# A two-layer attention and spectral kernel: who does the work at a layer's end, in which order ScalarE runs the loop, and when weights are split

## The chip, the cores and the metric

The kernel runs on one core of a Trainium2 chip. The metric is the device time of one execution in microseconds (us), as the median of several runs. The engines are PE (TensorE, matmuls), DVE (VectorE), ACT (ScalarE), POOL (GpSimd) and SP (SyncE, which here issues the DMAs).

## What is computed

Two layers, each an attention block and then a spectral block, both with a layer norm ahead and a residual added. The sequence has 2048 rows, the model 1024 columns, 32 heads of 32 columns.

```python
def _A_ref(x, wqkv, wo):                      # attention
    qkv = (x @ wqkv).reshape(B, S, 3, H, Dh) ...
    scores = einsum("bhqd,bhkd->bhqk", q, k) * (Dh ** -0.5)
    p = softmax(scores)
    o = einsum("bhqk,bhkd->bhqd", p, v)
    return o.transpose(...).reshape(B, S, D) @ wo
def _B_ref(x, w_r, w_i):                      # spectral filter
    X = rfft2(x) * (w_r + 1j * w_i)
    return irfft2(X)
x = A_x
for _ in range(2):
    x = x + _A_ref(_layernorm(x), A_wqkv, A_wo)
    x = x + _B_ref(_layernorm(x), B_w_r, B_w_i)
```

## The kernel before, in words

**Precision.** Matmuls of projections and scores take f16 pairs: a value is split into hi (ScalarE, a scaled cast, L166) and lo (VectorE, the rest, L167), and three products hi·hi, hi·lo, lo·hi are summed. `split` (L164) does both.

**The prologue of a layer** normalizes 16 tiles of 128 rows (`ln_tile`), transposes and splits them into `big`, and projects the first V, K and Q groups.

**The loop** (L608 on) runs over 8 groups g of four heads, 4 chunks c of 512 queries, 16 key tiles kt. A step computes the scores of four heads into two PSUM tiles (`S`, L540) and two exponentials of 128x1024 (L544, ScalarE). Every second step multiplies two tiles of exponentials into the output (`PV`, L550). VectorE adds the exponentials up (`add`, L561 and L563), since the sums are the softmax's denominators. After a chunk's last key tile `fin` sums over partitions (L569, PE), transposes, takes reciprocals and scales the output (L570 to L576, VectorE), and at kt = 5 of the next chunk `out` casts it (L582, ScalarE), takes the rest (L583, GpSimd) and stores both halves to `od` in DRAM (SP).

**Beside it** the projections of the next groups fill PE's free time: `filler` (L386) yields in slices, and each sum, of 24 matmuls (`qk_chunk`, L327) or more (`v_tiles`, L371), ends with a split or a copy. A phase's weights are loaded and split by `prep` (L231): slices of 256 KB by DMA into a buffer of three (`wst`), two slices for a Q or K group, four for a pair of V groups. Each is split (L253) and in layer 0 also searched for its largest magnitude (L256, L257, VectorE). `filler` advances `prep` by one slice behind each sum. In the last two groups the filler is the output projection: `load_wo` splits `wo` in 16 slices (into `big`), `wo_parts` computes the first 7 of 8 groups' part of the rows.

**Who sets the order.** PE's order in the loop and at the layer's end is that of the source (`manual_schedule`, L607). The other engines' instructions are put in order by a scheduler at build time, which may move a cast or a weight split ahead of exponentials that stand before it in the source. Engines then run their instructions strictly in that order.

**The layer's end** (L656 on). Rows 0 to 1535 (tiles 0 to 11) have their last eighth added in `wo_rest`, whose statistics are gathered in `mvs`; `fold_rests` normalizes them all. The last chunk's four tiles (`first`, `last`) wait for the loop's last `fin` and `out`: their last eighth is multiplied by `olast`. Each normalized tile is folded: sums and differences of its two halves of rows' columns (`fold`, L141; two operations of 128x8x8x8, GpSimd), ready for the first transposes of the spectral block (`t1`, L742). The inverse root of the variance (`ln_scale`, L116) is one power on GpSimd (L120) and five small operations on VectorE, one of them ahead of the power (L119), four behind (a Newton step, L121 to L124). `norm_folded` then normalizes the folded tile in two halves (L160, L161; VectorE). So for tiles 0 to 11: 24 folds on GpSimd, 24 halves normalized on VectorE.

**The flags.** In layer 1 the kernel reduces its range flags over all partitions (`partition_all_reduce`, L1088, GpSimd), an operation whose code is not resident: GpSimd's order has an exchange of code before and after it. The same holds for the largest norms of each group in the loop (L352).

Of the kernel before, what the change touches and what calls it, by code (L numbers as in the profile page):

```python
# [6 lines left out]
F32 = mybir.dt.float32  # L7
# [4 lines left out]
AF = mybir.ActivationFunctionType  # L12
ALU = mybir.AluOpType
# [99 lines left out]
    return st  # L113


def ln_scale(nc, sm, cst, mv, n=1):  # L116

    v, r, q = (sm.tile([128, n], F32, name=f"{c}{n}") for c in "vrn")
    nc.vector.tensor_scalar(v, mv[:, 1::2], 1e-5, None, op0=ALU.add)  # L119
    nc.gpsimd.tensor_tensor(r, v, cst["mhalf"].broadcast_to([128, n]), op=ALU.pow)  # L120
    nc.vector.tensor_mul(q, r, r)  # L121
    nc.vector.tensor_mul(q, q, v)
    nc.vector.tensor_scalar(q, q, -0.5, 1.5, op0=ALU.mult, op1=ALU.add)
    nc.vector.tensor_mul(r, r, q)  # L124
    return r


def ln_stats(nc, sm, cst, st, mv):

    nc.vector.bn_aggr(mv, st)  # L130
    return ln_scale(nc, sm, cst, mv)


def layernorm(nc, sm, cst, x, out):
# [3 lines left out]
    nc.vector.tensor_scalar(out, x, mv[:, 0:1], r, op0=ALU.subtract, op1=ALU.mult)  # L138


def fold(nc, x, out, a):  # L141

    xv = x.rearrange("p (a u g q) -> p g a u q", a=8, g=2, q=8)[:, :, a]
    ov = out.rearrange("p (u g a q) -> p g a u q", g=2, a=8, q=8)[:, :, a]
    nc.gpsimd.tensor_tensor(ov[:, 0], xv[:, 0], xv[:, 1], op=ALU.add)
    nc.gpsimd.tensor_tensor(ov[:, 1], xv[:, 0], xv[:, 1], op=ALU.subtract)


def fold_norm(nc, sm, cst, st, out):

    mv = sm.tile([128, 2], F32, name="mv")
    r = ln_stats(nc, sm, cst, st, mv)
    b = sm.tile([128, 1], F32, name="b")
    nc.vector.tensor_scalar(b, mv[:, 0:1], 2.0, None, op0=ALU.mult)
    norm_folded(nc, out, out, b, r)


def norm_folded(nc, x, out, b, r):
    xv, ov = (a.rearrange("p (u g q) -> p g u q", g=2, q=64) for a in (x, out))
    nc.vector.tensor_scalar(ov[:, 0], xv[:, 0], b, r, op0=ALU.subtract, op1=ALU.mult)  # L160
    nc.vector.tensor_scalar(ov[:, 1], xv[:, 1], r, None, op0=ALU.mult)  # L161
# [8 lines left out]
def run(g):  # L170
    for _ in g:
        pass
# [89 lines left out]
SPILL = [2, 3, 8, 9]  # L262
# [3 lines left out]
def attention(nc, tc, layer, ap, xin, yd, wts, wo, cst, dram, flags):  # L266
# [5 lines left out]
    pp, qp, sgp, wqp, wvp = ap.pp, ap.qp, ap.sgp, ap.wqp, ap.wvp  # L272
    sq, on, on2, sm = ap.sq, ap.on, ap.on2, ap.sm
# [14 lines left out]
    V, K, Q, bias, nrm, mx = {}, {}, {}, {}, {}, {}  # L288
# [106 lines left out]

# [68 lines left out]
    wo_dst = [ap.x[:, 10 + t if t in SPILL else t] for t in range(8)] + [None] * 2 + [ap.x[:, t] for t in (10, 11)]  # L464
# [12 lines left out]
    mvs = sm.tile([128, 24], F32, name="mvs")  # L477

    def wo_rest(t):
        p = psS.tile([128, 2, 512], F32, name="s")  # L480
        nc.vector.bn_aggr(mvs[:, 2 * t:2 * t + 2], wo_last(t // 4, t % 4, p, wo_dst[t], wo_dst[t], True))
# [12 lines left out]

    vk = [v_tiles(PH0[0], t) for t in range(8)]
    xn = [ln_tile(0), ln_tile(1)]
# [14 lines left out]
    for c in range(NCH):  # L511
        t = 4 * c + 4
# [91 lines left out]
                yield sums - (i + m >= steps)  # L604
            sums -= 1

    with tc.manual_schedule(engines={mybir.EngineType.PE}):  # L607
        for g in range(NG):  # L608
            todo = sum(sums(ph) for ph in beside.get(g, []))
            sl = slots(fill, todo, 22 if g == NG - 2 else 32, 24)  # L610
# [1 line left out]
            for u in range(NCH * NKT):  # L612
# [26 lines left out]
                elif g == NG - 1:  # L639
                    t = rests[0] if rests else 16  # L640
# [15 lines left out]
        run(wof)  # L656
        for t in rests:
            wo_rest(t)
        ps, xs = [], []
# [16 lines left out]
        fold_rests()  # L676
        first(1, range(7))
        last(0)
        first(2, range(7))
        last(1)  # L680
        first(3, range(4))
        last(2)
        first(3, range(4, 7))
        last(3)
# [494 lines left out]
```

## Time and profile before

| what | us |
|---|---|
| median of 3 runs (lowest, highest) | 4022.38 (4021.28, 4024.88) |
| the profiled execution's own time | 4029.87 |
| its span, first to last instruction | 4028.0 |
| layer 0: loop, end | 130 to 1680, 1680 to 1760 |
| layer 1: loop, end | 2130 to 3675, 3675 to 3762 |

The mean granted TensorE clock is 0.982. PE's busy time in stretches is 1502.4 of 1545 us in layer 1's loop, 52.8 of 80 us at layer 0's end and 54.7 of 87 us at layer 1's end. A row of a timeline gives the start, the duration, the engine, the line, the operation, output and inputs, and in brackets the engine's idle time before it and what ended that. A row of a view of waits gives an engine, the tile and line that it was about to work on, the engine, tile and line that it waited for, and total, number and longest of the waits. A row of a view by line gives total and mean (ns) behind the bar, then the idle time before them.

### The profile page before, as it was taken

The numbers are of one execution on the slowest core, as the hardware profiler recorded it, in microseconds if no ns is written. First come the engines' busy times: TensorE is split into PE (matmuls) and PEld (weight loads), VectorE is DVE, ScalarE is ACT, GpSimd is POOL, SyncE is SP. The second block draws the span as 40 slices with busy tenths as digits, with TensorE's granted clock in tenths as the row PEclk, the third lists the DMA queues.
The fourth block names the chain that finished last, engine by engine and source line by source line (L and its number), as shares of the span: only waits on it lengthen the run. The fifth ranks groups of instructions, "written<-read, shape, count | busy, mean of one in ns | idle before, by whom it ended". The sixth has DMA issues, their size and how long they took to land. (4 is left out here: it accounts for less than half of the span.)

```text
span 4028.0 us, 80149 instructions
## 1 busy us (share of the span) xinstructions
PE 3791.8 (94%) x33204; PEld 1680.2 (42%) x33204; DVE 3257.1 (81%) x3897; ACT 2863.0 (71%) x3533; POOL 634.9 (16%) x585
## 2 busy tenths in 40 slices
PE   7999999999999999979989999999999999997898
PEld 5322423342234233368854234233422432332787
DVE  6789888888988977766766898888889889788456
ACT  4677777787778866448746787788878888663485
POOL 1111011101110100314321110111011101003143
PEclk9999999999999999989989999999999999999999
DMA  3000000000000211143120000000000002121333
GB/s 114 19 22 17 7 22 14 14 9 22 17 12 7 87 51 66 53 152 125 57 84 14 27 17 7 22 17 14 7 22 17 12 9 87 53 72 49 141 101 100
DMA packets 97561, 177.32 MB, mean 44 GB/s; under 512 B 7201, under 2 KB 52897, under 8 KB 96161
## 3 DMA queue, kind: packets, MB, share of 16 engines
q1 hardware_dynamic: 97040, 172.03, 12.7%
q8 instruction: 262, 4.29, 0.5%
q14 instruction: 115, 0.93, 0.1%
q10 hardware_dynamic: 144, 0.07, 0.0%
HBM read 123.83 MB, written 48.23 MB: 43 GB/s over the span
## 5 line engine op out<-in xcount | busy, mean ns | idle before, releaser
L544 ACT ACTIVATE p<-s,bias 128x1024 f32<-128x1024 f32 x2048 | 2163.9, 1111 | 534.6 <-PE s L540 527.9
L563 DVE TENSOR_TENSOR R<-R,p 128x1024 f32<-128x1024 f32 x1792 | 2163.1, 1259 | 163.2 <-ACT p L544 160.7
L550 PE MATMUL o<-p,R 128*32 128x512 f32 x8192 | 996.0, 604 | 0.0
L327 PE MATMUL x<-big,wqk 128*128 128x512 f16 x2880 | 678.6, 380 | 18.0 <-DVE R L167 9.3
L540 PEld LDWEIGHTS <-R 32*128 32x128 f16 x12288 | 239.1, 92 | 845.6 <-issue 728.6
L540 PE MATMUL s<-R 32*128 32x512 f16 x6144 | 444.4, 380 | 49.2 <-ACT p L544 44.4
L540 PE MATMUL s<-Q,R 32*128 32x512 f16 x6144 | 442.2, 378 | 27.8 <-ACT p L544 16.7
L327 PEld LDWEIGHTS <-wqk 128*128 128x128 f16 x3072 | 276.8, 98 | 449.1 <-issue 162.8
L550 PEld LDWEIGHTS o<-p,R 128*32 128x32 f32 x8192 | 214.8, 109 | 529.7 <-issue 529.1
L371 PEld LDWEIGHTS <-big 128*128 128x128 f16 x3072 | 291.9, 98 | 102.3 <-issue 56.3
L371 PE MATMUL x<-wv,big 128*128 128x256 f16 x2688 | 321.1, 275 | 5.9 <-DVE big L167 2.9
L561 DVE SCALAR_TENSOR_TENSOR R<-p 128x1024 f32<-128x1024 f32 x128 | 153.9, 1204 | 195.6 <-ACT p L544 195.6
L331 POOL TENSOR_TENSOR sq<-R 128x512 bf16<-128x512 f16 x96 | 149.3, 1555 | 970.8 <-ACT R L166 970.6
L583 POOL TENSOR_TENSOR ohl<-zt,ohl 128x512 f16<-128x512 f32 x62 | 83.2, 1342 | 1178.4 <-ACT ohl L582 1178.4
L429 PE MATMUL x<-big 128*128 128x512 f16 x1008 | 228.0, 380 | 0.0
L429 PEld LDWEIGHTS <-big 128*128 128x128 f16 x1344 | 126.8, 98 | 177.6 <-issue 35.4
L582 ACT CAST ohl<-zt 128x512 f16<-128x512 f32 x64 | 39.6, 618 | 140.0 <-DVE zt L576 98.6
L861 DVE TENSOR_TENSOR H<-G,H 128x512 f16<-128x512 f32 (+1 forms) x68 | 46.7, 687 | 104.1 <-ACT H L860 104.0
L331 POOL TENSOR_TENSOR sq<-Q 128x512 bf16<-128x512 f16 x32 | 48.9, 1529 | 444.6 <-ACT Q L166 444.6
L813 PE MATMUL ps<-cbi,H 128*128 128x256 f16 (+1 forms) x792 | 99.1, 273 | 5.6 <-ACT H L860 3.7
L806 ACT COPY U<-ps 64x256 f32<-64x256 f32 (+1 forms) x272 | 97.0, 357 | 7.8 <-PE ps L813 2.6
L806 ACT COPY B<-ps 64x256 f32<-64x256 f32 (+1 forms) x272 | 97.0, 356 | 6.7 <-PE ps L813 2.4
(417 smaller groups left out, 3256.3 us busy)
## 6 DMA issues: line engine op xcount, KB each, us to landing
wst<-in_wp SPq DMA_DIRECT2D x96, 256.0 KB, 2.8
R<-y SPq DMA_DIRECT2D x32, 512.0 KB, 5.2
w<-in_w SPq DMA_DIRECT2D x60, 256.0 KB, 2.7
od<-ohl SPq DMA_DIRECT2D x56, 256.0 KB, 2.4
big<-od SPq DMA_DIRECT2D x16, 896.0 KB, 6.4
y<-R SPq DMA_DIRECT2D x20, 512.0 KB, 2.6
R<-in_x SPq DMA_DIRECT2D x16, 512.0 KB, 6.8
wst<-in_wo SPq DMA_DIRECT2D x32, 256.0 KB, 3.1
```

Of the source, the lines that this page charges most:

```text
L327: nc.tensor.matmul(ps, a, b, start=d == 0 and i == 0, stop=d == 7 and i == 2)
L331: nc.gpsimd.tensor_tensor(nrm[ph][:, c], t[:, 0], t[:, 0], op=ALU.mult)
L371: nc.tensor.matmul(ps[:, j], l, r, start=d == 0 and i == 0, stop=d == 7 and i == 2)
L429: nc.tensor.matmul(p, a, b, start=start and d == ds[0] and i == 0, stop=stop and d == ds[-1] and i == 2)
L540: nc.tensor.matmul(s[h // 2][:, h % 2], K[g][r, a, kt * 128:kt * 128 + 128], Q[g][r, b, c * 512:c * 512 + 512], start=i == 0, stop=i == 2)
L544: nc.scalar.activation(p, s[hf], AF.Exp, bias=bias[g], scale=SCALE / (SQ * SQ))
L550: nc.tensor.matmul(O[g, c][32 * h:32 * h + 32], V[g][:, kt, 32 * h:32 * h + 32], P[g, c, kt, h // 2][:, h % 2], start=kt == 0, stop=kt == ...
L561: nc.vector.scalar_tensor_tensor(acc[hf], P[g, c, 0, hf], 1e-34, p, op0=ALU.add, op1=ALU.add)
L563: nc.vector.tensor_add(acc[hf], acc[hf], p)
L583: eng.tensor_tensor(t[:, 1], r, t[:, 0], op=ALU.subtract)
L806: nc.scalar.copy(ov[64 * r:64 * r + 64, a0:a0 + m, x], tl[64 * x:64 * x + 64, :m, r])
L813: nc.tensor.matmul(out, l, r, start=k == 0, stop=k == len(mm_) - 1)
```

## The change

Four things change.

1. `ln_scale` takes the engine. At a layer's end all its operations, with two more for the bias (`scale_bias`), run on GpSimd: eight small ones per call.
2. At a layer's end ScalarE normalizes a whole tile (L498, 128x1024) and VectorE folds the result; for the last four tiles VectorE folds first, then ScalarE normalizes one half (L685) and VectorE the other (L686). `fold_rests` is a generator: six tiles come before `first(1)`, four behind `last(0)`, the rest behind `last(1)`, as far as ScalarE's and VectorE's order goes by the source (PE's alone does at the layer's end).
3. In the loop ScalarE, too, runs in the order of the source: `manual_schedule` takes Activation.
4. Behind the second and each later sum of a phase `filler` advances `prep` twice instead of once, so that splits come in pairs, and a phase's last one comes one sum or more sooner.

```diff
-def ln_scale(nc, sm, cst, mv, n=1):
+def ln_scale(nc, sm, cst, mv, eng, n=1):
     v, r, q = (sm.tile([128, n], F32, name=f"{c}{n}") for c in "vrn")
-    nc.vector.tensor_scalar(v, mv[:, 1::2], 1e-5, None, op0=ALU.add)
+    eng.tensor_scalar(v, mv[:, 1::2], 1e-5, None, op0=ALU.add)
     nc.gpsimd.tensor_tensor(r, v, cst["mhalf"].broadcast_to([128, n]), op=ALU.pow)
...
-def fold(nc, x, out, a):
+def fold(nc, x, out, a, eng=None):
...
             for n in range(sums(ph)):
                 yield from (v_tiles if ph[0] == "v" else qk_chunk)(ph, n)
-                next(nxt, None)
+                for _ in range(1 + (n > 0)):
+                    next(nxt, None)
...
+    def scale_bias(mv, n, m):
+        r = ln_scale(nc, sm, cst, mv, nc.gpsimd, n)
+        b = sm.tile([128, n], F32, name=f"b{n}")
+        nc.gpsimd.tensor_tensor(b, mv[:, 0::2], r, op=ALU.mult)
+        nc.gpsimd.tensor_scalar(b, b, -m, None, op0=ALU.mult)
+        return r, b
+
     def fold_rests():
-        r = ln_scale(nc, sm, cst, mvs, 12)
-        b = sm.tile([128, 12], F32, name="b12")
-        nc.vector.tensor_scalar(b, mvs[:, 0::2], 2.0, None, op0=ALU.mult)
+        r, b = scale_bias(mvs, 12, 1.0)
         for t in SPILL + [t for t in range(12) if t not in SPILL]:
-            o = ap.x[:, t]
-            f = o if t in SPILL else pp.tile([128, 1024], F32, name="xn", tag="p")
-            fold(nc, wo_dst[t], f, slice(0, 8))
-            norm_folded(nc, f, o, b[:, t:t + 1], r[:, t:t + 1])
+            f = pp.tile([128, 1024], F32, name="xn", tag="p")
+            nc.scalar.activation(f, wo_dst[t], AF.Identity, bias=b[:, t:t + 1], scale=r[:, t:t + 1])
+            fold(nc, f, ap.x[:, t], slice(0, 8), nc.vector)
+            yield
...
-    with tc.manual_schedule(engines={mybir.EngineType.PE}):
+    with tc.manual_schedule(engines={mybir.EngineType.PE, mybir.EngineType.Activation}):
...
+    with tc.manual_schedule(engines={mybir.EngineType.PE}):
+        ps, xs, folds = [], [], fold_rests()
...
         def last(t):
             o = ap.x[:, 12 + t]
             st = wo_last(3, t, ps[t], xs[t], xs[t], False)
-            fold(nc, xs[t], o, slice(0, 8))
-            fold_norm(nc, sm, cst, st, o)
+            mv = sm.tile([128, 2], F32, name="mv")
+            nc.vector.bn_aggr(mv, st)
+            r, b = scale_bias(mv, 1, 2.0)
+            fold(nc, xs[t], o, slice(0, 8), nc.vector)
+            ov = o.rearrange("p (u g q) -> p g u q", g=2, q=64)
+            nc.scalar.activation(ov[:, 0], ov[:, 0], AF.Identity, bias=b, scale=r)
+            nc.vector.tensor_scalar(ov[:, 1], ov[:, 1], r, None, op0=ALU.mult)
```

Lines behind the first edits have higher numbers in the new kernel (L166 is L167, L544 is L552, L582 is L590, L145 is L146, L570 is L578, L1088 is L1108).

PE's order is the same in both. On ScalarE, in layer 0's loop, where the four splits of the first V weights (`wv`) of the loop stood before (p is a tile of exponentials, x8 means eight in a row, oc and ohl are a chunk's output):

```order
L166 ACTIVATE wqk<-wst 128x512 x2
L544 ACTIVATE p<-s,bias 128x1024 x2
L166 ACTIVATE wv<-wst 128x4x128
L544 ACTIVATE p<-s,bias 128x1024 x2
L166 ACTIVATE wv<-wst 128x4x128
L544 ACTIVATE p<-s,bias 128x1024 x2
L166 ACTIVATE wv<-wst 128x4x128
L544 ACTIVATE p<-s,bias 128x1024 x2
L166 ACTIVATE wv<-wst 128x4x128
L544 ACTIVATE p<-s,bias 128x1024 x4
```

and where they stand now:

```order
L167 ACTIVATE R<-x 128x512
L552 ACTIVATE p<-s,bias 128x1024 x4
L167 ACTIVATE wv<-wst 128x4x128 x2
L552 ACTIVATE p<-s,bias 128x1024 x6
L562 COPY oc<-o 128x512
L552 ACTIVATE p<-s,bias 128x1024 x2
L167 ACTIVATE R<-x 128x512
L552 ACTIVATE p<-s,bias 128x1024 x4
L167 ACTIVATE wv<-wst 128x4x128 x2
L552 ACTIVATE p<-s,bias 128x1024 x4
L590 CAST ohl<-zt 128x512
```

The four splits followed one pair of `wqk` splits within eight exponentials; now they come in two pairs, each four exponentials behind the end of a sum (R<-x), and nearly a group later. Likewise the pair of splits of the first K weights of the loop, which the scheduler had put into the prologue, now stands behind the loop's first four exponentials.

On VectorE at layer 0's end, around the last chunk's `fin` before (xn and R hold tiles, b and r their bias and root):

```order
L160 TENSOR_SCALAR R<-xn,b_18278,r_18270 128x8x64
L161 TENSOR_SCALAR R<-xn,r_18270 128x8x64
L570 STREAM_TRANSPOSE zt<-s 128x512
L160 TENSOR_SCALAR R<-xn,b_18278,r_18270 128x8x64
L572 RECIPROCAL rc<-zt 128x16
L161 TENSOR_SCALAR R<-xn,r_18270 128x8x64
L573 TENSOR_TENSOR fr<-fr,rc 128x16
L575 STREAM_TRANSPOSE zt<-rc 128x512
L160 TENSOR_SCALAR R<-xn,b_18278,r_18270 128x8x64
L576 SCALAR_TENSOR_TENSOR zt<-oc,zt 128x512
```

and now:

```order
L146 TENSOR_TENSOR R<-xn 128x8x8x8
L147 TENSOR_TENSOR R<-xn 128x8x8x8
L578 STREAM_TRANSPOSE zt<-s 128x512
L146 TENSOR_TENSOR R<-xn 128x8x8x8
L580 RECIPROCAL rc<-zt 128x16
L147 TENSOR_TENSOR R<-xn 128x8x8x8
L581 TENSOR_TENSOR fr<-fr,rc 128x16
L583 STREAM_TRANSPOSE zt<-rc 128x512
L146 TENSOR_TENSOR R<-xn 128x8x8x8
L584 SCALAR_TENSOR_TENSOR zt<-oc,zt 128x512
```

The transpose stood behind 16 halves of a norm (eight tiles), the first of which waited for the root; it now stands behind ten folds (five tiles). Twelve VectorE operations, eleven folds and the lo part of the cast, stand between the product with zt and the first of the last four tiles.

On GpSimd at layer 1's end before (ISA without operands is an exchange of code, fa the flags):

```order
L146 TENSOR_TENSOR xn<-R 128x8x8x8
L1088 ISA
L1088 ISA fa<-f_43236 128x6
L145 ISA
L145 TENSOR_TENSOR R<-xres 128x8x8x8
L146 TENSOR_TENSOR R<-xres 128x8x8x8
L120 TENSOR_TENSOR r_39957<-v_39956,mhalf 128x1
```

and now:

```order
L489 TENSOR_TENSOR b_39935<-mv,r_39927 128x1
L490 TENSOR_SCALAR b_39935<-b_39935 128x1
L1108 ISA
L1108 ISA fa<-f_43236 128x6
L119 ISA
L119 TENSOR_SCALAR v_40016<-mv 128x1
L120 TENSOR_TENSOR r_40017<-v_40016,mhalf 128x1
```

The flags' reduction stood behind the folds of tiles 0 to 11 and ahead of the first of the last four tiles; it now stands between the small operations of the first and of the second of these four. SP's order changes in the same stretch: stores of the last tiles stand between other loads of the spectral block's constants than before.

More of the change, by code (lines that the diff above doesn't have):

```diff
@@ L113, in bn_stats @@
     return st
-def ln_scale(nc, sm, cst, mv, n=1):
+def ln_scale(nc, sm, cst, mv, eng, n=1):
     v, r, q = (sm.tile([128, n], F32, name=f"{c}{n}") for c in "vrn")
-    nc.vector.tensor_scalar(v, mv[:, 1::2], 1e-5, None, op0=ALU.add)
+    eng.tensor_scalar(v, mv[:, 1::2], 1e-5, None, op0=ALU.add)
     nc.gpsimd.tensor_tensor(r, v, cst["mhalf"].broadcast_to([128, n]), op=ALU.pow)
[L121 to L124, printed above, removed]
+    eng.tensor_tensor(q, r, r, op=ALU.mult)
+    eng.tensor_tensor(q, q, v, op=ALU.mult)
+    eng.tensor_scalar(q, q, -0.5, 1.5, op0=ALU.mult, op1=ALU.add)
+    eng.tensor_tensor(r, r, q, op=ALU.mult)
     return r
@@ L670, in last, with some @@
             st = wo_last(3, t, ps[t], xs[t], xs[t], False)
-            fold(nc, xs[t], o, slice(0, 8))
-            fold_norm(nc, sm, cst, st, o)
+            mv = sm.tile([128, 2], F32, name="mv")
[5 more added lines that the diff above has]
+            nc.vector.tensor_scalar(ov[:, 1], ov[:, 1], r, None, op0=ALU.mult)
+        def some(n):
+            for _ in range(n):
+                next(folds, None)
         first(0, range(7))
@@ L675, in attention @@
         out(NG - 1, NCH - 1, nc.vector)
-        fold_rests()
+        some(6)
         first(1, range(7))
         last(0)
+        some(4)
         first(2, range(7))
         last(1)
+        run(folds)
         first(3, range(4))
```

8 lines of the change are left out of this document (4 added, 4 removed).

## The prediction

> **What bounds the kernel now.** I read the page first, then the waits of PE and ACT over each attention loop, then timelines at the places these named. The page's first lines:
>
> ```profile
> span 4028.0 us, 80149 instructions
> PE 3791.8 (94%) x33204; PEld 1680.2 (42%) x33204; DVE 3257.1 (81%) x3897; ACT 2863.0 (71%) x3533; POOL 634.9 (16%) x585
> ```
>
> PE is the bound. Its 54144-instruction order is the same in both kernels, so only PE's idle time, 4028.0 − 3791.8 = 236 us, is to be had. The waits of PE over layer 0's loop (130 to 1680 us; columns: engine, what it was about to do, whom it waited for, total, times, longest):
>
> ```profile
> PE s L540 <- ACT p L544: 31.0, 29, 4.7
> PE s L540 <- DVE mqk L346: 11.3, 7, 3.5
> ```
>
> and over layer 1's loop (2130 to 3675 us):
>
> ```profile
> PE s L540 <- ACT p L544: 29.1, 28, 3.5
> PE s L540 <- DVE mqk L346: 2.8, 4, 0.8
> ```
>
> So 60.1 us go while a score matmul waits for an exponential. What held ScalarE is in its own waits over layer 0's loop:
>
> ```profile
> ACT wv L166 <- DMA wst<-in_wp: 29.8, 12, 5.3
> ACT ohl L582 <- DVE zt L576: 11.8, 8, 3.8
> ```
>
> ScalarE stands in front of a V-weight split whose slice has not landed, and the exponentials queue behind it.
>
> **Part A, the V-weight splits.** One such place, in the timeline at 200 us (start, duration, engine, line, in brackets the idle time and its releaser):
>
> ```profile
> 199.72 0.63 ACT L166 ACTIVATE wv<-wst 128x512 f16<-128x512 f32 x1 [3.75 <-DMA wst<-in_wp]
> 201.40 1.86 PE L540 MATMUL s<-R 32*128 32x512 f16 x12 [3.15 <-ACT p L544]
> ```
>
> ScalarE waits 3.75 us, PE loses 3.15. Six such bursts occur, three in each layer; PE's waits in 25 us around each (195, 575, 960, 2215, 2587 and 2960 us):
>
> ```profile
> PE s L540 <- ACT p L544: 6.4, 3, 3.1
> PE s L540 <- ACT p L544: 5.0, 2, 3.3
> PE s L540 <- ACT p L544: 6.6, 3, 4.7
> PE s L540 <- ACT p L544: 4.8, 3, 3.2
> PE s L540 <- ACT p L544: 5.2, 3, 3.5
> PE s L540 <- ACT p L544: 6.4, 4, 3.5
> ```
>
> Together 34.4 us. In the new order each V split stands where a sum ends, and by the two orders at least 28 exponentials separate the freeing of a staging buffer from the use of what is loaded into it: 29 us by the four in 4.12 us quoted in part C, where the longest wait for a slice was 5.3. I take the whole −34.4. The DMA's own queue is SP, where the load stands behind an `od` store that waits for the cast six exponentials later than before; 28 exponentials cover that, too. The output-weight splits (`big`, last burst of a layer) have only 4 to 12 exponentials of cover: 0, between −3 and +3.
>
> **Part B, the casts.** In the source order a cast stands at kt = 5 again, behind 44 exponentials of its chunk instead of 38. Before, three times in a layer this reached PE:
>
> ```profile
> 426.72 0.82 PE L540 MATMUL s<-Q,R 32*128 32x512 f16 x10 [0.97 <-ACT p L544]
> ```
>
> Six times 0.97 is 5.8; I take −5.
>
> **Part C, what the loop gets instead.** K1's pair of splits leaves the prologue, where PE had enough to do, and stands behind the loop's first four exponentials. Before, at the start of layer 0's loop:
>
> ```profile
> 127.98 0.27 POOL L357 TENSOR_SCALAR bias<-bpr 128x1 f32<-128x1 f32 x1
> 129.89 4.12 ACT L544 ACTIVATE p<-s,bias 128x1024 f32<-128x1024 f32 x4 [0.18 <-PE s L540]
> 131.81 1.90 PE L327 MATMUL x<-big,wqk 128*128 128x512 f16 x8
> 133.04 2.36 DVE L561 SCALAR_TENSOR_TENSOR R<-p 128x1024 f32<-128x1024 f32 x2 [11.91 <-ACT p L544]
> ```
>
> The first K1 matmul, at 131.81, must now wait for the hi part on ScalarE (134.01 + 0.6) and the lo part on VectorE behind L561 (135.40 + 0.7, as L167 takes beside this, = 136.1). That is 4.3 us later; I take +4 a layer, +8, from 0 (if the matmuls' f16 hi half starts sooner) to 10. Pairs of splits in place of single ones hold exponentials up by 1.2 instead of 0.63 us, twelve times, each mostly inside ScalarE's slack: +2, up to 6. Two prologue pairs less give at most −2 back; not counted.
>
> **Part D, layer 0's end.** The chain of the end, with what each row shows:
>
> ```profile
> 1694.43 0.21 DVE L481 BATCH_NORM_AGGREGATE mvs<-st 128x2 f32<-128x12 f32 x1
> 1707.67 2.31 POOL L120 TENSOR_TENSOR r<-v,mhalf 128x12 f32<-128x12 f32 x1
> 1710.02 1.22 DVE L121 TENSOR_TENSOR n<-r 128x12 f32<-128x12 f32 x1 [14.38 <-POOL r L120]
> 1722.61 0.70 DVE L570 STREAM_TRANSPOSE zt<-s 128x512 f32<-128x512 f32 x1
> 1726.05 0.62 ACT L582 CAST ohl<-zt 128x512 f16<-128x512 f32 x1 [38.16 <-DVE zt L576]
> 1726.72 2.74 PE L429 MATMUL s<-big,ohl 128*128 128x512 f16 x6 [20.18 <-ACT ohl L582]
> 1752.37 1.22 DVE L458 SCALAR_TENSOR_TENSOR xres<-s,xres 128x1024 f32<-128x1024 f32 x1
> 1758.13 1.98 PE L742 MATMUL ps<-ident,R 128*128 128x128 f32 x8 [6.57 <-DVE R L160]
> ```
>
> GpSimd reached the root only at 1707.67, behind its folds; VectorE waited 14.38 us for it, normalized eight tiles, and only then did the last chunk's transpose at 1722.61. PE waited 20.18. Now GpSimd does nothing else. Prices, from the groups by line (total, mean ns):
>
> ```profile
> L354 POOL TENSOR_TENSOR bpr<-mall 128x1 f32<-128x1 f32 x16 | 6.7, 418 | 115.0 <-issue 115.0
> L357 POOL TENSOR_SCALAR bias<-bpr 128x1 f32<-128x1 f32 x16 | 9.5, 593 | 1.5
> L120 POOL TENSOR_TENSOR r<-v,mhalf 128x1 f32<-128x1 f32 x40 | 22.0, 550 | 75.2 <-ACT xn L303 42.4 <-DVE v L119 12.6 <-DVE fw L257 11.0
> L303 ACT ACTIVATE xn<-R,b,r 128x1024 f32<-128x1024 f32 x32 | 39.1, 1238 | 35.8 <-DVE b L301 21.8 <-DVE n L123 13.8
> L942 DVE TENSOR_TENSOR R<-R,sd 128x512 f32<-128x512 f32 x2 | 2.0, 1015 | 0.0
> ```
>
> The means of L354 and L357 hold ones that stood beside busy VectorE work; the undisturbed one in part C took 0.27. Eight GpSimd operations on 12 columns: 2.31 for the root and seven at about 0.3, 4.7 us (8.5 at most, by 0.6 to 0.9 each). From 1694.64 this gives 1699.4. ScalarE then normalizes a tile in 1.13 to 1.24, VectorE folds each in two operations. A fold here is 512 elements with runs of eight; the strided L942 row says 1.0, half of a dense 1024 (L561 in part C, two in 2.36) says 0.6. I take 0.6, since the runs are 32 bytes, and keep 1.0 for the range. Five tiles at 1.2 from 1700.6: 1706.7. The transpose, reciprocal, second transpose and product with three folds between them: 4.1, so zt at 1710.8, the cast 0.62, PE at 1711.7 instead of 1726.72: −15.0.
>
> From the restart to the first transpose of the next stage it was 1758.13 − 1726.72 = 31.4. The last tile's path (product to transpose 1758.13 − 1752.37 = 5.76) becomes product 1.2, statistics and half a fold 1.9, aggregate 0.2, eight small GpSimd operations 2.7 (0.55 and seven at 0.3), a half normalized 0.55, some 0.2 of handing over: 6.8. So +1; the layer's end gains 14. With folds of 1.0 each it gains 15 − 5 × 0.8 − 1.6 for the folds inside the chain − 3 × 0.8 for the four late tiles, that is 7, and with slow GpSimd operations 4.
>
> The Trainium skill ("SBUF — State Buffer", section "SBUF: two separate sides") says that VectorE and GpSimd share one port pair, held by an exclusive lock for a whole instruction. The trace agrees where it can: L121's 128x12 operation took 1216 ns beside GpSimd's folds, and GpSimd now meets VectorE's folds only in the small operations of the last tiles. By that rule each of these could wait out a 0.6 us fold; on the last tile one fold is left to meet, and the sum would be 0.6 worse.
>
> **Part E, layer 1's end.**
>
> ```profile
> 3721.39 2.74 PE L429 MATMUL s<-big,ohl 128*128 128x512 f16 x6 [20.17 <-ACT ohl L582]
> 3724.85 1.22 DVE L458 SCALAR_TENSOR_TENSOR xres<-s,xres 128x1024 f32<-128x1024 f32 x1
> 3736.88 1.25 POOL L145 TENSOR_TENSOR R<-xres 128x512 f32<-128x512 f32 x1 [12.55 <-DMA sg<-in_sg]
> 3759.27 1.97 PE L742 MATMUL ps<-ident,R 128*128 128x128 f32 x8 [11.99 <-DVE R L160]
> ```
>
> The same −15 at the restart. Behind it stands the all-reduce of the flags, and around it GpSimd's code is exchanged twice: the L145 fold's operand was ready at 3726.1 (L458), its 12.55 of idle time end at 3736.9, and I read them as the exchange back. The way there was over before and hidden. In the new order both ways lie between the small operations of tile 0 and those of tile 1. Tile 0's chain ends, counted from the restart R: twelve operations of 0.6 left on VectorE behind zt (eleven folds and the lo cast) 7.2, product 1.2, statistics and half a fold 1.9, aggregate 0.2, GpSimd 2.7, less the 0.9 from zt to R: 12.3. From L354's row one exchange in the loop is 115.0/16 = 7.2. So tile 1's chain starts between R + 12.3 + 14.8 = R + 27 and, with two of 12.55, R + 38. Behind its start: its chain 2.7, a half normalized, half the statistics, a fold and an aggregate 2.0 on VectorE, tile 2's chain 2.7, and tile 3's path of 6.8 with 0.5 ahead of it, 14.7: the first transpose at R + 42 to R + 53, where it was R + 37.9. The gain is 15 − 4 = 11 to 0; I take 6, midway, since 7.2 is a mean of sixteen and 12.55 stood in this very place. The Trainium skill ("GPSIMD Engine Reference", 2.1 "Instruction dispatch") puts the first call of freshly loaded code at about 6 us; by that the two would cost 12 and the gain would be 13.
>
> **The sum.** −34.4 − 5 + 8 + 2 + 0 − 14 − 6 = −49.4. The profiled execution took 4029.87, 1.9 above its span and 7.5 above the median of 4022.38; I take the difference from the median: **3973 us**.
>
> **The rivals.**
> 1. *GpSimd's exchange eats layer 1's gain.* Both exchanges at 12.55, and three late chains slowed by 2 each by VectorE's folds: layer 1's end loses 6 instead of gaining 6, the total is −37: 3985. For it: the 12.55. Against: 7.2 in the loop. Chance 0.15.
> 2. *Folds on VectorE take 1.0 to 1.25 each* so layer 0's end gains 4, layer 1's loses 6, and part A brings only 80% since the lumps take the rest: −34.4 × 0.8 − 5 + 10 + 2 − 4 + 6 = −18: 4004. For it: L942. Chance 0.12.
> 3. *Slower: VectorE becomes the bound in the loop.* In layer 0 every pair of splits brings VectorE two splits and two maxima in one lump:
>
> ```profile
> L167 DVE SCALAR_TENSOR_TENSOR wqk<-wst,wqk 128x512 f16<-128x512 f32 x24 | 18.4, 803 | 0.0
> L256 DVE TENSOR_REDUCE wm<-wst 128x1 f32<-128x512 f32 x33 | 22.3, 683 | 11.5 <-DMA wst<-in_wp 11.4
> ```
>
> A lump is 2 × (0.80 + 0.68 + 0.2) = 3.4 in layer 0 and 1.6 in layer 1, where there are no maxima; 20 pairs a layer (24 and 12 splits of `wqk` and `wv`, and four out of the prologue) make 68 + 32 = 100 us if PE waits them all out, because adds free the exponentials' buffers. It decides the sign from half of that, since the other terms bring 49; all of it would be 4022 + 51 = 4073. For it: the wait behind `mqk`, 11.3 in layer 0 against 2.8. Against: wqk pairs stand together before as well, and PE's waits for VectorE in layer 0 are 11.3 + some 10. Chance 0.07.
> 4. *It doesn't do what it says*: by the order the transpose still stands behind ten folds on VectorE, and if ScalarE's normals start late (their tiles are shared with the last exponentials' buffers) the stall at the end stays, and the new pairs stall where the old ones did: within 8 us of 4022. Chance 0.08.
>
> My forecast has 0.58. A measurement of this kernel tells about 0.2% (8 us) from no change. Range: the low end takes D at 16, E at 11, C and the pairs at 0: −49.4 − 2 − 5 − 10 = −66, 3956; the high end takes rival 2 with a slow `big` split (+3) and the pairs at 6 (+4): −11, 4011. Faster 0.87, same 0.06, slower 0.07.
>
> **What would show it.** In the new profile: no rows of the V splits waiting for `wst`, and PE's waits for exponentials at 20 to 25 us in a layer instead of 31; a new wait of about 4 us before the first K1 matmul of each layer; the L146 and L147 folds at 0.6 to 0.7 on VectorE; the wait before the last chunk's output matmuls at some 5 us instead of 20; and in layer 1 a gap on GpSimd between two chains of 14 to 25 us. I am wrong if the V splits still wait, if PE's waits for VectorE grow by more than 20 us a layer, or if the folds take over 1 us.

## The result and the profile after

The changed kernel takes 3956.72 us (median of 4 runs, 3952.66 to 3958.57) where the kernel before takes 4023.23 beside it: a ratio of 0.9834, 95% interval 0.9816 to 0.9851, or 66.5 us less. Run again beside the last experiments it came to 3959.07 against 4027.95, 0.9822 (0.9807 to 0.9837). Forecast were 3973 and 49 us, with a range from 3956 to 4011, so the measured time lies just inside its low end. The changed kernel's profiled execution is the fastest of the four, while that of the kernel before, 4029.87, lies above all four of its runs, so the two spans differ by 77 us; about 10 of these are scatter. Two executions among the runs below, of 6150 and 4218 us at a mean granted clock of 0.56 and 0.88, are left out of the medians.

The stages, by the starts and ends of rows in the two timelines (a layer's loop runs from its first score matmul to the end of the last `mvs` aggregate, the restart is the first matmul on `ohl`):

| stage | before | after | change | forecast |
|---|---|---|---|---|
| layer 0's loop | 1565.7 | 1535.2 | −30.5 | about −15 |
| its end up to PE's restart | 32.1 | 16.6 | −15.5 | −15 |
| restart to first transpose | 31.4 | 35.9 | +4.5 | +1 |
| layer 1's loop | 1538.7 | 1515.3 | −23.3 | about −15 |
| its end up to PE's restart | 32.1 | 16.6 | −15.5 | −15 |
| restart to first transpose | 37.9 | 41.9 | +4.1 | +4 to +15 |

How much of a loop is waiting: the two loops before (stretch, its length, PE's busy time and number of matmuls, then the other engines; granted clock third from the end),

```profile
130.00:1690.00 1560.00, 1502.00 (x13616) 515.52 (x13616) 1360.71 (x1370) 1182.64 (x1243) 166.30 (x122) 0.99 0.08 27
2150.00:3685.00 1535.00, 1492.60 (x13638) 514.52 (x13637) 1337.38 (x1304) 1183.40 (x1245) 171.54 (x124) 1.00 0.08 28
```

and after:

```profile
128.00:1659.00 1531.00, 1490.17 (x13624) 512.14 (x13623) 1355.21 (x1382) 1184.21 (x1249) 169.45 (x115) 0.99 0.08 29
2107.00:3618.00 1511.00, 1483.29 (x13624) 510.33 (x13622) 1327.33 (x1308) 1184.12 (x1249) 225.41 (x115) 0.99 0.09 29
```

PE's idle time fell from 58.0 to 40.8 and from 42.4 to 27.7, by 32 us together; the forecast had 29. But its busy time fell as well, by 11.8 and 9.3 us, with as many matmuls. That was in no term of the sum. Where it came from is taken up behind the doses below.

What PE waits for in layer 0's loop now (in the kernel before: 31.0 for exponentials, 11.3 for `mqk`, some 10 for VectorE's halves of splits):

```profile
PE s L548 <- ACT p L552: 13.1, 13, 6.7
PE x L328 <- DVE R L168: 6.7, 4, 2.3
PE x L328 <- DVE Q L168: 6.3, 3, 2.2
PE x L372 <- DVE R L168: 6.0, 3, 2.1
```

The wait for `mqk` is down to 1.9. ScalarE's own waits list no split of V weights that waits for its slice any more, and no cast. Half of what is left of the wait for exponentials is one wait of 6.7. In layer 1's loop the waits for exponentials are 12.0, again with one of 6.7, and three waits of 2.2 for GpSimd's squares (`sq`, L332) are new.

The loop's start, with the wait that part C expected:

```profile
133.00 1.16 ACT L167 ACTIVATE wqk<-wst 128x512 f16<-128x512 f32 x2
133.70 0.61 PE L328 MATMUL x<-big,wqk 128*128 128x512 f16 x2 [2.71 <-ACT wqk L167]
134.44 1.29 DVE L168 SCALAR_TENSOR_TENSOR wqk<-wst,wqk 128x512 f16<-128x512 f32 x2
135.17 2.74 PE L328 MATMUL x<-big,wqk 128*128 128x512 f16 x6 [0.87 <-DVE wqk L168]
```

Layer 0's end, the rows that answer to those shown of before:

```profile
1663.01 0.21 DVE L483 BATCH_NORM_AGGREGATE mvs<-st 128x2 f32<-128x12 f32 x1
1663.65 2.31 POOL L120 TENSOR_TENSOR r<-v,mhalf 128x12 f32<-128x12 f32 x1
1667.49 0.27 POOL L490 TENSOR_SCALAR b<-b 128x12 f32<-128x12 f32 x1
1667.79 2.38 ACT L498 ACTIVATE xn<-R,b,r 128x1024 f32<-128x1024 f32 x2 [9.26 <-POOL b L490]
1669.07 0.69 DVE L146 TENSOR_TENSOR R<-xn 128x512 f32<-128x512 f32 x1 [5.85 <-ACT xn L498]
1679.12 0.60 ACT L590 CAST ohl<-zt 128x512 f16<-128x512 f32 x1
1679.78 0.61 PE L431 MATMUL s<-big,ohl 128*128 128x512 f16 x2 [2.59 <-ACT ohl L590]
1708.53 1.23 DVE L460 SCALAR_TENSOR_TENSOR xres<-s,xres 128x1024 f32<-128x1024 f32 x1 [2.00 <-DMA xres<-in_x]
1715.72 2.01 PE L762 MATMUL ps<-ident,R 128*128 128x128 f32 x8 [10.23 <-ACT R L685]
```

The root starts 0.4 us behind the last statistics (1663.65 behind 1663.22) instead of 13.0, the chain on GpSimd ends 4.5 us behind them, folds follow each other every 0.60 us, and PE waits 2.59 us instead of 20.18. And layer 1's end:

```profile
3639.09 0.60 PE L431 MATMUL s<-big,ohl 128*128 128x512 f16 x2 [2.60 <-ACT ohl L590]
3658.60 0.40 POOL L1108 PARTITION_ALL_REDUCE fa<-f  x1 [6.90 <-issue]
3667.13 0.25 POOL L119 TENSOR_SCALAR v<-mv 128x1 f32<-128x1 f32 x1 [8.13 <-issue]
3681.03 2.01 PE L762 MATMUL ps<-ident,R 128*128 128x128 f32 x8 [16.26 <-ACT R L685]
```

The two exchanges of GpSimd's code stand in the open, 6.9 and 8.1 us, and tile 1's chain starts at 28.0 us behind the restart.

### The profile page after: what moved, and what is told of

Same layout as the page of the kernel before. It is cut to its first block, busy times and chain, and to the rows that moved or that the text cites. A ratio compares the mean times of both kernels' runs of the same rounds, so it can differ in the third digit from the quotient of the medians.

```text
span 3950.8 us, 80100 instructions
## 1 busy us (share of the span) xinstructions
PE 3770.9 (95%) x33204; PEld 1671.8 (42%) x33204; DVE 3225.5 (82%) x3845; ACT 2893.9 (73%) x3565; POOL 643.4 (16%) x591
## 3 DMA queue, kind: packets, MB, share of 16 engines
q1 hardware_dynamic: 97040, 172.03, 12.7%
## 4 chain that ended last, share of the span: by engine, by line
PE 76%; DVE 9%; issue 7%; ACT 4%; POOL 3%; DMA 1%; SPq 0%; DVEq 0%; ACTq 0%; POOLq 0%
PE o L558 21%; PE s L548 17%; PE x L328 13%; PE x L372 8%; PE x L431 6%; DVE R L571 2%; ACT p L552 2%; PE ps L833 2%; PE ps L771 2%; PE s L577 1%; PE o L372 1%; PE ps L762 1%; PE ps L948 1%; PE o L328 1%; PE ps L902 1%
## 5 line engine op out<-in xcount | busy, mean ns | idle before, releaser
L552 ACT ACTIVATE p<-s,bias 128x1024 f32<-128x1024 f32 x2048 | 2168.3, 1111 | 585.0 <-PE s L548 573.8
L558 PE MATMUL o<-p,R 128*32 128x512 f32 x8192 | 985.0, 598 | 0.0
L328 PE MATMUL x<-big,wqk 128*128 128x512 f16 x2880 | 686.6, 384 | 22.7 <-DVE R L168 8.2
L548 PEld LDWEIGHTS <-R 32*128 32x128 f16 x12288 | 231.1, 92 | 781.1 <-issue 664.8
L328 PEld LDWEIGHTS <-wqk 128*128 128x128 f16 x3072 | 277.6, 98 | 460.7 <-issue 169.4
L548 PE MATMUL s<-R 32*128 32x512 f16 x6144 | 431.9, 379 | 19.0 <-ACT p L552 15.5
L548 PE MATMUL s<-Q,R 32*128 32x512 f16 x6144 | 432.0, 378 | 11.9 <-ACT p L552 10.6
L591 POOL TENSOR_TENSOR ohl<-zt,ohl 128x512 f16<-128x512 f32 x62 | 180.0, 2903 | 1473.4 <-ACT ohl L590 1473.4
L332 POOL TENSOR_TENSOR sq<-R 128x512 bf16<-128x512 f16 x96 | 142.4, 1483 | 703.0 <-ACT R L167 702.5
L332 POOL TENSOR_TENSOR sq<-Q 128x512 bf16<-128x512 f16 x32 | 45.1, 1409 | 321.3 <-ACT Q L167 321.3
L833 PE MATMUL ps<-cb,big 128*128 128x256 f16 x780 | 96.3, 273 | 0.0
```

The lines of the kernel that those rows point to most:

```text
L328: nc.tensor.matmul(ps, a, b, start=d == 0 and i == 0, stop=d == 7 and i == 2)
L332: nc.gpsimd.tensor_tensor(nrm[ph][:, c], t[:, 0], t[:, 0], op=ALU.mult)
L548: nc.tensor.matmul(s[h // 2][:, h % 2], K[g][r, a, kt * 128:kt * 128 + 128], Q[g][r, b, c * 512:c * 512 + 512], start=i == 0, stop=i == 2)
L552: nc.scalar.activation(p, s[hf], AF.Exp, bias=bias[g], scale=SCALE / (SQ * SQ))
L558: nc.tensor.matmul(O[g, c][32 * h:32 * h + 32], V[g][:, kt, 32 * h:32 * h + 32], P[g, c, kt, h // 2][:, h % 2], start=kt == 0, stop=kt == ...
L591: eng.tensor_tensor(t[:, 1], r, t[:, 0], op=ALU.subtract)
```

## The experiments

**What each part is worth.** First the loop's edits alone, with the layer ends of before:

```diff
-                next(nxt, None)
+                for _ in range(1 + (n > 0)):
+                    next(nxt, None)
-    with tc.manual_schedule(engines={mybir.EngineType.PE}):
+    with tc.manual_schedule(engines={mybir.EngineType.PE, mybir.EngineType.Activation}):
...
+    with tc.manual_schedule(engines={mybir.EngineType.PE}):
         ps, xs = [], []
```

> The loop's edits alone (source order on ScalarE, splits in pairs), the layer ends as before. The prediction's sum gave the loop -29 us. Theory: the loop is worth more, since each wait of PE also costs a stretch at a lower granted clock behind it; the two loops of the changed kernel are 30.5 and 23.3 us shorter in the profiles, so 4023 - 54 = 3969, with about 10 us of doubt from single executions: 3965 to 3980. Rival: the loop brings the 29 of the sum and the ends the rest, 3994.

3986.37 beside 4027.01: a ratio of 0.9895 (0.9881 to 0.9909), 40.6 less. It lies between the two numbers, outside the range given for the theory: more than the sum's 29, but 13 less than the 54 of the two profiles, since that of the changed kernel had caught a fast loop. Over the profiles of all kernels with this same loop, layer 0's takes 1535.2 to 1544.1 us at nearly the same waits.

Then the changed kernel without the source order on ScalarE:

```diff
-    with tc.manual_schedule(engines={mybir.EngineType.PE, mybir.EngineType.Activation}):
+    with tc.manual_schedule(engines={mybir.EngineType.PE}):
```

> The changed kernel without the source order on ScalarE; its splits come in pairs in the source, but ScalarE's and VectorE's order in the loop is again that of the kernel before, row for row, so that this run is also the layer ends alone. Theory: the ends bring 15.5 - 4.5 and 15.5 - 4.1, 22 us together: 4023 - 22 = 4001; the V splits wait for their slices again (some 30 us on ScalarE in layer 0) and PE's granted clock falls behind each. Rival: the ends bring 37, what the sum of the prediction leaves if the loop is worth 29: 3986.

3999.45, a ratio of 0.9930 (0.9912 to 0.9947), 27.6 less, and the splits stall as before (ScalarE's waits in layer 0's loop, this run):

```profile
ACT wv L167 <- DMA wst<-in_wp: 27.4, 12, 4.6
```

So pairs in the source do nothing while a scheduler orders ScalarE. The two runs, 40.6 and 27.6, add up to the 66.5 to 69 of the whole. The layer ends account for 22 of the 27.6 by the profiles, as the theory had it; in this run's profile the two loops, in the order of before, are 4.6 shorter as well.

Third, ScalarE in source order, but one split behind each sum:

```diff
-                for _ in range(1 + (n > 0)):
-                    next(nxt, None)
+                next(nxt, None)
```

> The changed kernel with one split behind each sum instead of two, ScalarE in source order. A V phase's last slice is then split right before its first matmul. Theory: three V phases a layer wait 2 to 4 us each for that, and the clock behind it: 10 to 25 us more than the changed kernel, 3967 to 3982. Rival: the pairs are what makes VectorE late (nine waits of about 2 us in layer 0 of the changed kernel), and single splits take most of them away: 10 us less, 3947.

3986.93, 0.9895 (0.9881 to 0.9910): some 27 us more than the changed kernel, and above the 3967 to 3982 expected. Its waits of PE in layer 0's loop:

```profile
PE x L372 <- DVE wv L168: 13.9, 3, 4.6
...
PE x L328 <- DVE R L168: 7.9, 6, 1.6
PE x L372 <- ACT wv L167: 7.2, 3, 2.4
PE x L328 <- DVE Q L168: 4.8, 3, 1.9
```

A V phase has four slices and the phase ahead of it four sums, of which one slot goes to the loading; the fourth split then stands right ahead of its first use, and PE waits 7.0 us three times in layer 0. The lumps on VectorE are a cost of the pairs, as the rival has it, but a smaller one: PE's waits for VectorE's halves of sums are 7.9 + 4.8 = 12.7 here and 19.0 in the changed kernel.

**What a wait costs.** Ten, then twenty tiny copies on ScalarE at one place of each chunk, whose result nobody reads:

```diff
+    scr = sm.tile([128, 16], F32, name="scr")
...
+                if kt == 11:
+                    for _ in range(10):
+                        nc.scalar.copy(scr, ident[:, 0:16])
```

> The changed kernel with ten tiny copies (128x16, into a scratch tile that nobody reads) on ScalarE at key tile 11 of each of the 64 chunks: some 2 us of ScalarE time ahead of the next exponentials, of which ScalarE's own slack of about 0.8 us takes a part. Theory (a wait costs PE more than itself only where it is long, by the lower granted clock behind it): PE waits some 1.2 us in 64 places, the clock behind stays near 1.0, 77 us more than the changed kernel. Rival (a wait costs itself, whatever its length): the same 77.

> The same with twenty copies, some 4 us. Theory: PE waits 3.2 us in 64 places, 205 us, and runs for some 8 us at a granted clock of 0.5 to 0.8 behind each, as in the kernel before at 200 to 210 us, worth 2 to 3 us each: 330 to 400 us more than the changed kernel. Rival: only the waits, 205 us more, and the clock in the loop stays at 0.98 to 1.0.

The ten, 2.3 us of ScalarE, cost 4025.74 − 3959.07 = 66.7 us, 1.0 for each of 64; the twenty, 4.7 us, cost 315.3, 4.9 each: twice the dose, 4.7 times the price, a little less than the theory's 330 to 400 and far more than the rival's 205. The ten stayed below the 77 that both had. PE's waits for exponentials from 140 to 1640 us (31 such places, and 29 with twenty copies) and this stretch, with ten copies

```profile
PE s L549 <- ACT p L553: 35.0, 38, 7.2
140.00:1640.00 1500.00, 1447.04 (x13180) 497.81 (x13175) 1300.47 (x1322) 1199.71 (x1520) 158.27 (x114) 0.99 0.08 27
```

and with twenty:

```profile
PE s L549 <- ACT p L553: 98.6, 31, 8.1
140.00:1640.00 1500.00, 1382.23 (x12272) 473.64 (x12272) 1202.31 (x1218) 1186.77 (x1719) 151.08 (x112) 0.95 0.07 21
```

Against the 11.0 of the changed kernel in this stretch, ten copies make PE wait 0.8 us in each place at an unchanged clock of 0.99, twenty 3.0 us at 0.95. Most of the other 1.9 us of the 4.9 are matmuls at a lower clock. One of the places, with the clock from 324 to 330 us:

```profile
325.27 1.46 PE L549 MATMUL s<-R 32*128 32x512 f16 x10 [3.52 <-ACT p L553]
326.66 4.59 PE L328 MATMUL x<-big,wqk 128*128 128x512 f16 x12
```

```profile
324.00:330.00 6.00, 4.73 (x18) 1.47 (x18) 5.32 (x5) 4.34 (x5) 1.04 (x1) 0.50 0.00 0
```

The length of a wait does not settle whether that happens. The same twelve L328 matmuls at the same place in two executions of the changed kernel, the profiled one and that of its second run, behind nearly the same wait:

```profile
247.90 2.75 PE L328 MATMUL x<-big,wqk 128*128 128x512 f16 x12 [2.17 <-DVE Q L168]
```

```profile
247.70 4.44 PE L328 MATMUL x<-big,wqk 128*128 128x512 f16 x12 [2.14 <-DVE Q L168]
```

In these two profiles the loops have 21 waits of 1.9 to 2.4 us; behind 10 of them the granted clock falls to 0.5 for 3.4 us, and a stretch like that costs 1.7 us.

**Where PE's time in the loops goes.** The clock can be taken out of the busy time: busy time × (1 − granted clock), added up over short windows, is what the lower clock cost, and the rest is busy time at full clock. For the two loops of a profile together (a pause is an idle time of PE of more than 0.15 us):

| kernel | idle | lower clock | busy at full clock | pauses |
|---|---|---|---|---|
| before | 100.4 | 17.5 | 2986 | 122 |
| changed | 68.5 | 14.4 | 2968 | 64 |
| changed, second run | 68.7 | 27.2 | 2966 | 64 |
| the loop's edits alone | 69.1 | 23.5 | 2970 | 63 |
| no source order on ScalarE | 96.9 | 22.8 | 2980 | 118 |
| ten copies | 111.9 | 19.4 | 2989 | 131 |
| twenty copies | 262.1 | 134.3 | 2977 | 131 |

The changed loop loses 14 to 27 us to the clock where the loop before lost 17.5, so the theory of the run of the loop alone, that a lower clock behind each wait explains the extra gain, is refuted by its own trace: it loses 23.5. What fell is the busy time at full clock, by 10 to 21 us according to which runs are compared, together with the number of pauses. The rows of the kernel before show what a pause does to a step's twelve score matmuls, first without one, then with one behind the second matmul:

```profile
133.64 0.83 PE L540 MATMUL s<-R 32*128 32x512 f16 x12
```

```profile
2230.40 0.39 PE L540 MATMUL s<-R 32*128 32x512 f16 x2
2231.26 0.82 PE L540 MATMUL s<-R 32*128 32x512 f16 x10 [0.48 <-ACT p L544]
```

In one piece the twelve are busy for 0.83 us, broken in two for 0.39 + 0.82 = 1.21: a matmul that has nothing to overlap with adds 0.38 us of busy time to the wait of 0.48. An estimate from this, 58 pauses fewer at 0.38, is 22 us. The ten copies bear it out from the other side: 67 pauses more than in the second run of the changed kernel, 43 us more idle time, 8 less at a lower clock, and 23 more busy at full clock, 0.34 for each. With twenty copies the idle time grows by 193 and the lower clock costs 107 more, 1.7 for each of 64 places; there the split between clock and pauses is rough, since the two coincide.

**The wait of 6.7 that is new.** Its chain in the changed kernel:

```profile
1343.16 9.31 POOL L591 TENSOR_TENSOR ohl<-zt,ohl 128x512 f16<-128x512 f32 x1 [9.80 <-ACT ohl L590]
1352.50 0.38 SPq L593 DMA_DIRECT2D od<-ohl  x1
1352.97 0.91 SPq L408 DMA_DIRECT2D wst<-in_wo  x2
1355.77 0.63 ACT L167 ACTIVATE big<-wst 128x512 f16<-128x512 f32 x1 [6.61 <-DMA wst<-in_wo]
```

The lo half of a cast took 9.31 us on GpSimd, where its mean was 1.34 in the kernel before and is 2.90 in this one, while VectorE ran adds and splits without a gap; the store waits for it, the loads stand behind the store on SP's queue, and the split on ScalarE holds the exponentials. In layer 1 three more casts, of 8.1 us each, stand ahead of the squares for which PE now waits 2.2 us. The first try moved the cast of another chunk:

```diff
-                    out(*done.pop())
+                    d = done.pop()
+                    out(*d, nc.vector if d == (NG - 2, 0) else nc.gpsimd)
```

> The changed kernel with the lo half of one cast per layer (the one whose store stands ahead of the output weights' loads) on VectorE instead of GpSimd. There it took 9.3 us in the profile, and the store, the loads behind it on SP's queue, the split on ScalarE and PE (6.7 us) waited for it one behind the other. Theory: both waits of 6.7 us go, and with them the lower clock behind them, 3 to 5 us each: 4 to 12 us more is lost to nothing, so 3957 - 20 = 3937, between 3933 and 3945. Rival: the loads are late for themselves (three buffers of 256 KB), the wait stays within 2 us of 6.7, and the time stays at 3957.

3955.99, 0.9820 (0.9808 to 0.9833), as the changed kernel; the lo half that matters was still on GpSimd (9.16 us) and PE waited 7.05. With `(NG - 2, 1)`:

> As the run before it of this kind, which moved the cast of another chunk; now the one whose store stands ahead of the output weights' loads in the last but one group (9.2 us on GpSimd, from 1352.9, in that run's profile, and PE waiting 7.05 behind it). Theory: GpSimd's lo half holds up the store, the loads behind it on SP, the split on ScalarE and PE; with the lo half on VectorE the wait of 6.6 to 7.0 us in each layer shrinks to under 2, and the low clock behind it goes too: 12 to 20 us less than the changed kernel, a ratio to the kernel before of 0.979 to 0.981 instead of 0.9834. Rival: the loads are late for themselves, 256 KB each with three buffers, and the wait stays above 5 us: 0.983.

```profile
1351.11 0.69 DVE L591 TENSOR_TENSOR ohl<-zt,ohl 128x512 f16<-128x512 f32 x1
1351.83 0.38 SPq L593 DMA_DIRECT2D od<-ohl  x1
1355.72 0.63 ACT L167 ACTIVATE big<-wst 128x512 f16<-128x512 f32 x1 [1.00 <-DMA wst<-in_wo]
```

3950.13, 0.9809 (0.9796 to 0.9822). The split waits 1.00 instead of 6.61, and PE 1.1 and 1.8 in layer 0 and 2.1 in layer 1 instead of 6.7: the chain was as read. The time is some 5 to 10 us less, below the 12 to 20 expected, and its interval overlaps that of the changed kernel.

**Three smaller repairs.** These, and the one above, ran beside the kernel before and not beside the changed kernel, so their few us to the latter's 3956.72 and 3959.07 are between different chips; what they do is read from their traces. The flags' all-reduce held back into the spectral block:

```diff
+        if late is not None and (g, i) == (0, 1):
+            nc.vector.scalar_tensor_tensor(late, tt[:, 0, 0:16], 0.0, late, op0=ALU.mult, op1=ALU.max)
```

> The changed kernel with the flags' all-reduce held back until the second tile of layer 1's spectral block is transposed (a 128x16 operation on VectorE more), where GpSimd has nothing to do for 55 us. Theory: the exchanges of GpSimd's code (6.9 and 8.1 us) are what makes layer 1's stretch from the restart of PE to the first transpose 41.9 us; it becomes layer 0's 35.9: 6 us less in the trace, and about 6 of 3957 in time. Rival: the late tiles are bound by something else in layer 1 too, and the stretch stays within 1 us of 41.9.

3951.3, 0.9803 (0.9788 to 0.9818). The restart is at 3648.56 and the first transpose now at

```profile
3682.46 2.01 PE L762 MATMUL ps<-ident,R 128*128 128x128 f32 x8 [8.13 <-ACT R L685]
3687.35 0.40 POOL L1110 PARTITION_ALL_REDUCE fa<-f  x1 [5.79 <-issue]
```

which is 33.9 us behind the restart instead of 41.9: the exchanges were what held the layer's end, and it is now 2.0 shorter than layer 0's, whose last product waits 2.00 us for its residual rows.

The first K pair back in the prologue:

```diff
     def filler():
-        run(prep(phases[0]))
...
+    run(prep(("k", 1)))
     for v in vk:
```

> The changed kernel with the first K pair of the loop split in the prologue again, as before the change. Theory (part C of the prediction): the waits of PE of 2.7 and 0.9 us at the loop's start go, and its first steps run 4.2 us earlier in each layer: 8 us less in all, 3949. Rival: the prologue takes the split's time instead and the sum is unchanged, 3957.

3948.83, 0.9803 (0.9788 to 0.9818), 8 to 10 less, and PE does not wait before the first K1 matmul:

```profile
130.60 1.90 PE L328 MATMUL x<-big,wqk 128*128 128x512 f16 x8
```

The residual rows of the last two tiles in buffers that are free:

```diff
-                xs.append(xres(3, t))
+                x = pp.tile([128, 1024], F32, name="xr", tag="p") if t > 1 else ...
```

> The changed kernel with the residual rows of the last two tiles loaded into two of the exponentials' buffers, which are free by then, instead of buffers that wait for the first tiles' stores. Theory: in layer 0 the last tile's product waited 2.0 us for these rows (landing 7.3 us after issue, behind constants), so that layer 0's stretch from restart to first transpose falls from 35.9 to about 33.9, and layer 1's stays at 41.9, since GpSimd is late there. Rival: the loads only trade places with the constants' and the stretch stays within 0.5 us.

3952.86, 0.9818 (0.9803 to 0.9833), no difference to the changed kernel that this can tell. The wait for the rows is gone, and layer 0's stretch still takes 35.5 instead of 35.9, since what stood behind these loads on SP came earlier as well: slices of `wo`, whose maxima (L757) VectorE now takes in between the last tiles, one of them right ahead of the third tile's statistics.

```profile
1704.53 0.68 DVE L757 TENSOR_REDUCE wom<-wo 128x1 f32<-128x512 f32 x1
1705.12 1.28 DVE L462 BATCH_NORM_STATS2 st<-xr 128x6 f32<-128x512 f32 x2
```

Layer 1's stretch came to 39.9; its exchanges took 6.1 and 6.9 us this time.

**All four together**, beside a second run of the changed kernel:

> The changed kernel itself once more, beside the next three on the same chip, so that they are compared with it and not only with the kernel before. Theory and rival: a ratio of 0.983 to 0.984 to the kernel before.

> The changed kernel with the four repairs together: the lo half on VectorE, the flags late, the K pair in the prologue, the residual rows early. Theory: they lie in different places and add up, 10 + 8 + 8 + 2 = 28 us less than the changed kernel, 3929 where that has 3957, a ratio of about 0.976 to the kernel before. Rival: they gain little beyond any one of them, since the single runs of each came out at about the same ratio (0.980 to 0.982), 0.980.

3928.86 (3920.74 to 3931.57), 0.9754 (0.9741 to 0.9768), against 3959.07 and 0.9822 for the changed kernel on the same chip: 30 us less where 28 were expected, so the repairs add up. It beats both kernels.

## Why the prediction was right, and where a size was off

The time came out 16 us below the forecast and 0.7 inside the range. That it lies inside is in part luck: the low end was reached by taking D at 16, E at 11, C and the pairs at 0, and in the runs D is 11, E 11, C was paid in full, and what made up for it was in no term. By the runs the loop gave 41 for 29 and the layer ends 22 to 28 for 20.

- **Part A, the V splits (−34.4), and part B, the casts (−5).** Right as waits: none is left, and PE's waits for exponentials fell from 61.0 to 25.1 us, by 35.9 for 39.4, with the two new waits of 6.7 in them. Wrong as a price. The step that failed is the premise that only PE's idle time is to be had: it takes the busy time as fixed, and each wait as costing its own length. In the run of the loop alone 31 us come from idle time and 16 from busy time at full clock, with 63 pauses for 122, and 6 are lost again to the clock: 42 by the profile, 41 by the run. Why a pause costs busy time is shown by the rows and the copies above; that this is all of the 16 is an estimate. The clock behind the long wait of the first burst in the kernel before, and behind that of the last:

```profile
200.00:205.00 5.00, 3.60 (x24) 0.93 (x27) 5.00 (x9) 3.70 (x5) 0.00 (x0) 0.53 0.15 52
205.00:210.00 5.00, 4.92 (x34) 1.14 (x27) 2.63 (x4) 1.32 (x3) 0.00 (x0) 0.78 0.18 56
2966.73:2976.73 10.00, 8.27 (x72) 2.50 (x75) 8.27 (x9) 6.22 (x7) 0.00 (x0) 1.00 0.25 79
```

  It is 0.53 and 0.78 behind the wait of 3.15 at 201.40, but 1.00 behind one of 3.52 at 2966.73. Behind the longest waits of the six bursts the lower clock cost 2.9, 2.9, 2.3, 1.7, 1.7 and 0, 11.5 us together; those are gone, and others have come, behind the waits of 6.7, of 2.7 at the loop's start and of some 2 for VectorE. The Trainium skill ("TensorE: Matmul & The Clock Gate", Part 1) puts the fall to half the clock behind an idle window of about 3.4 us. The runs agree in kind, in that slow matmuls followed five of these six waits and 10 of the 21 of about 2 us, but not in the limit: 2.08 and 2.14 us were enough in some places, and 3.52 were not in another.
- **The `big` splits (0, −3 to +3).** Outside the range: 6.7 us in each layer, where PE's waits for exponentials in that stretch made 4.0 and 3.7 before, so +5.7, and 2.9 of lower clock behind each 6.7. The cover was counted in exponentials from cast to split, without the 9.3 us that the cast's lo half takes on GpSimd beside VectorE's adds. The Trainium skill ("SBUF — State Buffer", "SBUF: two separate sides") has a port pair that VectorE or GpSimd holds for a whole instruction; the prediction used that section for the layer's end. It would fit, in that the cast ended 1.0 us behind the last of the adds, but the cast waited out several instructions and not one, and that the port is the cause was not tested.
- **Part C (+4 a layer).** Right: waits of 2.71 and 0.87, 3.6 together, and some slower matmuls behind; undoing it gave 8 to 10.
- **Part D, layer 0's end (−14).** The restart was right to 0.5 us (−15.5 for −15.0), with the GpSimd chain at 4.5 for 4.7 and folds at 0.60. Behind it the stretch grew by 4.5 instead of 1. The last product waits 2.0 for its residual rows (at 1708.53), which stand on SP behind other loads than before; with that wait taken away the stretch was still 35.5, since other work came in its place. Layer 1, without that wait and without exchanges, still shows 2.5 more, 33.9 for 31.4. A part of them lies in VectorE's half of each late tile (L686), which waits for the root ahead of the next tile's product; VectorE's waits at this end:

```profile
DVE R L686 <- POOL r L124: 7.4, 4, 1.9
```

- **Part E, layer 1's end (−6).** −11.4 by the profile. Both exchanges took 6.9 and 8.1 us, the lower end of the range (7.2), and the first transpose came at restart + 41.9, for which the forecast had 42 to 53; the value taken leaned on the 12.55 seen before, a row that names a DMA as what ended the idle time. Holding the flags back took 8.0 of them away. Rival 1 is refuted with it.
- **Rival 2** falls with folds of 0.60. **Rival 3**, lumps on VectorE, is there in small: PE waits 19 us for VectorE's halves in layer 0 instead of 10, 9 more, far from the 49 that a change of sign needs, and the shorter waits for `mqk`, 1.9 for 11.3, give that back. **Rival 4** is refuted as well: PE waits 2.59 us instead of 20.18 at the layer's end, and no V split waits; the pairs do need the source order for that.

## What to carry to other kernels

Price a pause of the bounding engine at more than its idle time: here each broke a run of overlapping matmuls, which cost some 0.3 to 0.4 us more, and behind half of the waits of about 2 us, and most of those over 3, came slow matmuls that cost 1.7 us or more. Count pauses beside adding up waits. A split or cast that can wait for a DMA should not stand in the queue of the engine that feeds the bound, and what is queued ahead of that DMA, down to a small GpSimd operation, counts as well. An operation whose code must be exchanged on GpSimd belongs where nothing waits for GpSimd.

## What was not expected of the hardware

A 128x512 operation with two inputs on GpSimd took 9.31 us beside VectorE's uninterrupted adds and ended 1.0 us behind the last of them, as did one of 8.07 in layer 1. In the kernel before the same operation took 1.42 us beside four adds in a row (at 333.00), and there the adds took 5.58 instead of 4.62: either engine can be the one that waits, and what decides stays open.

Two executions of the changed kernel differ by 8.6 us in layer 0's loop with nearly the same waits of PE. The lower clock cost 7.6 us in the one and 18.0 in the other, behind waits of the same length; what decides whether the clock falls behind a given wait stays open.
